# Attention followed by a two-layer MLP on one core: q and k turned by DMA for 33 pairs of heads, their loads moved from the SP queue to GpSimd's

## The chip, the cores and the metric

One core of one Trainium2 chip runs the whole program. The time is the device time of the program in microseconds (us). Three runs of the kernel before gave 479.93, 480.0 and 480.4 us, median 480.0 us. One more execution was profiled; all rows below come from it.

## The reference, cut to what matters

q, k and v are float32 of shape (8, 12, 448, 64): 8 batches, 12 heads, 448 positions, 64 columns.

```python
scores = (1/sqrt(64)) * q @ k^T
m = max(scores, -1);  e = exp(scores - m)
attn = e / (sum(e, -1) + exp(-m) + 1e-9)
x = (attn @ v), heads side by side      # (8*448, 768)
h = x @ w_in                            # (3584, 2048)
out = (h * tanh(softplus(h))) @ w_out   # (3584, 768), float32
```

## The kernel before, in words

**Pairs and units.** Work goes by pairs of heads: 48 pairs, 6 to a batch. Pairs 0 to 5 are a head part of their own (the loop `for p in range(HEAD)`, L618). From then on three pairs make a unit (`UNIT_PAIRS`, L16); the loop over units is L653, with u from 2 to 17. Unit u has the pairs p0 = 3u to 3u+2. Each unit has 12 steps (L664) and then 8 pieces of the first MLP matmul (the loop over f, L724).

**The life of a pair.** `load_pair` (L121) brings q, k and v of a pair from HBM, 224 KB each, as 112 partitions of 2 x 256 float32. `cast_pair` (L165) makes bfloat16 of q and k on GpSimd (L179, L180), `cast_v` (L185) of v (L188). `transpose_pair` (L190) turns q and k with eight TensorE instructions (L208, one block of 112 x 128 each) into PSUM. `evac_qk` (L221) takes them out: VectorE scales the two halves of q into `qd` (L254), ScalarE copies k into `kT` (L262). Then `scores` (L291): TensorE computes q k^T (L311), VectorE the negated maximum (L332), ScalarE the exponentials (`exps`, L345). `normalise` (L410) divides on VectorE, seven instructions a pair (L414), and turns the result `en` into `eT` with one DMA transpose on SP's queue (L422). `av_pair` (L445) multiplies by v on TensorE (L462) one unit later.

**MLP.** `mm1_mish` (L493) is the first layer with its activation, `mm2_part` (L523) the second, cut into chunks of two matmuls (L551) that fill the steps of the units from u = 4 on (`first_mm2`, L564). `store_rows` (L508) issues the output stores on SP's queue (L516).

**What sets the order.** The schedule is written out by hand: each engine executes its instructions in the order in which the program issues them, and so does each queue of DMAs. Within a unit:

- At the steps 0, 3 and 6 (`LOAD_AT`, L592) L689 to L694 load q and k of the pair four ahead (`LEAD` = 4, L591), load v of the next pair, cast q and k of the pair three ahead, and cast v of this pair. In the kernel before all these loads are on SP's queue, behind the DMA transposes and stores issued earlier.
- At the pieces f = 1, 3 and 5, L739 to L741 turn and evacuate q and k of the three pairs of the next unit. At f = 4, 6 and 7 the first three scores of the next unit are issued (L737, L742).
- At f = 0, 3 and 7, `normalise` divides the unit's three pairs and issues their three DMA transposes (L731, L744).
- `av_pair` of the last unit's three pairs goes with the last step of each pair (L305, L661).

**Weights.** `load_w` (L153) loads 20 pieces of w_in and w_out on GpSimd's queue, casting in the DMA. The last four pieces are issued in unit 4, after the steps 3, 5 and 7 (`W_AT`, L599). With `behind` it first makes GpSimd copy two elements (L157) that a pair's `eT` must hold, so that what follows waits for that DMA transpose.

**Times in the profile.** Unit 4 runs from about 97 to 123.51 us; unit 5 begins at 123.51, and each later unit 26.51 us after the last.

Of the kernel before, what the change touches and what calls it, by code (L numbers as in the profile page):

```python
# [10 lines left out]
BF16 = mybir.dt.bfloat16  # L11
# [4 lines left out]
UNIT_PAIRS = 3  # L16
# [3 lines left out]
def kernel(  # L20
# [9 lines left out]
    nc = tc.nc  # L30

    B, H, S, D = q.shape
# [3 lines left out]
    NT = 4  # L36
    SP_ = S // NT
    HP = H // 2
# [9 lines left out]
    N_PAIRS = B * HP  # L48
# [9 lines left out]
    PS = bass.MemoryType.PSUM  # L58
    singles = pool("singles", 1)
    ld_pool = pool("ld", 3)  # L60
    bf_pool = pool("bf", 4)
    qk_pool = pool("qk", 3)
    st_pool = pool("st", 5)
    hl_pool = pool("hl", 4)
    rb_pool = pool("rb", 2)
# [16 lines left out]
    w_in_sb = singles.tile([128, DM_T, d_ff], BF16)  # L82
    w_out_sb = singles.tile([128, FF_T, d_model], BF16)
    gT = singles.tile([128, FF_T, 2 * S], BF16)

    marks = singles.tile([1, 4, 16], BF16)
    N_EN = 5
# [30 lines left out]
    spread_copy = {}  # L118


    def load_pair(p, names="qkv"):  # L121
        if p >= N_PAIRS:
            return
        b, h0 = p // HP, (p % HP) * 2
        for nm in names:
            src = dict(q=q, k=k, v=v)[nm]
            t = ld_pool.tile([SP_, 2, NT * D], FP32, tag=f"{nm}_f", name=f"{nm}_f")
            nc.sync.dma_start(
                out=t, in_=src[b, h0 : h0 + 2].rearrange("h (p t) d -> p h (t d)", t=NT)
            )  # L130
            loaded.setdefault(p, {})[nm] = t
# [33 lines left out]
    def cast_pair(p, with_v=True):  # L165
        if p >= N_PAIRS:
            return
        q_f, k_f, v_f = (loaded[p].get(nm) for nm in "qkv")
        q_bf = bf_pool.tile([SP_, NT, 2, D], BF16, tag="q_bf", name="q_bf")
        k_bf = bf_pool.tile([SP_, NT, 2, D], BF16, tag="k_bf", name="k_bf")  # L170
        v_bf = bf_pool.tile([SP_, 2, NT * D], BF16, tag="v_bf", name="v_bf", bufs=12)
        by_t = "p h (t d) -> p t h d"
        q_t, k_t = (t.rearrange(by_t, t=NT) for t in (q_f, k_f))
        if p == 0:
            nc.vector.tensor_copy(out=k_bf, in_=k_t)
            for half in (slice(0, NT // 2), slice(NT // 2, NT)):
                nc.vector.tensor_copy(out=q_bf[:, half], in_=q_t[:, half])
        else:
            nc.gpsimd.tensor_copy(out=q_bf, in_=q_t)  # L179
            nc.gpsimd.tensor_copy(out=k_bf, in_=k_t)  # L180
        casted[p] = (q_bf, k_bf, v_bf)
        if with_v:
            cast_v(p)

    def cast_v(p):  # L185
        if p >= N_PAIRS:
            return
        nc.gpsimd.tensor_copy(out=casted[p][2], in_=loaded.pop(p)["v"])  # L188

    def transpose_pair(p, bank=None):  # L190
        if p >= N_PAIRS:
            return
        q_bf, k_bf, _ = casted[p]
        if bank is None:
            ps = mo_take()
            ps_k = mo_take() if p == 0 else ps
        else:
            ps, ps_k = sc_tiles[2 - bank][:, 0, :], sc_tiles[2 - bank][:, 1, :]
        by_s = [
            t[:, :].bitcast(BF16).rearrange("p (s n) -> p s n", s=2)[:, s, :]  # L200
            for s, t in enumerate((ps, ps_k))
        ]
        by_2 = sc_tiles[2][:, 0, :].bitcast(BF16)
        srcs = list(enumerate((q_bf, k_bf)))
        for s, src in reversed(srcs) if p == 0 else srcs:
            for t in range(NT):
                to = by_2 if p == 0 and s == 0 and t >= NT // 2 else by_s[s]
                nc.tensor.transpose(  # L208
                    to[:, t * SP_ : (t + 1) * SP_],
                    src[:, t].rearrange("p h d -> p (h d)"),  # L210
                    ident[:SP_, :SP_],
                )
        own = [] if bank is not None else [ps, ps_k] if p == 0 else [ps]
        qkT[p] = (by_s, own)
# [6 lines left out]
    def evac_qk(p, act=False):  # L221
        if p >= N_PAIRS:
            return
        (q_ps, k_ps), own = qkT[p]
        mo_free.extend(own)
        q_reads = []
        qd = q_diag[p % 3]
        kT = qk_pool.tile([128, S], BF16, tag="kT", name="kT")
        if p < DIAG_FROM:
            qT = qd.rearrange("d i h r -> d (i h r)")[:, 0:S]  # L230
            qkT[p] = (qT, kT)
            if p == 0:
                nc.scalar.copy(kT, k_ps[:, 0:S])
                by_2 = sc_tiles[2][:, 0, :].bitcast(BF16)
                for ps, half in (q_ps, slice(0, S // 2)), (by_2, slice(S // 2, S)):
                    nc.vector.tensor_scalar(
                        out=qT[:, half], in0=ps[:, half], scalar1=SCALE, scalar2=None,
                        op0=ALU.mult,
                    )
                return  # L240
            if act:
                nc.scalar.mul(qT, q_ps[:, 0:S], SCALE)
            else:
                q_reads.append(nc.vector.tensor_scalar(
                    out=qT, in0=q_ps[:, 0:S], scalar1=SCALE, scalar2=None, op0=ALU.mult
                ))
        else:
            qkT[p] = (qd, kT)
            if p < DIAG_FROM + 3:
                nc.vector.memset(qd[0:64, :, 1, :], 0.0)  # L250
                nc.vector.memset(qd[64:128, :, 0, :], 0.0)
            for h in range(2):
                rows = slice(64 * h, 64 * h + 64)
                q_reads.append(nc.vector.tensor_scalar(  # L254
                    out=qd[rows, :, h, :],
                    in0=q_ps[rows, 0:S].rearrange("d (i r) -> d i r", i=QB),
                    scalar1=SCALE, scalar2=None, op0=ALU.mult,
                ))
        if own and not act:
            nc.vector.tensor_copy(out=kT, in_=k_ps[:, 0:S])  # L260
        else:
            k_read = nc.scalar.copy(kT, k_ps[:, 0:S])  # L262
            if not own:
                apart(k_read, *q_reads)
# [326 lines left out]
    LEAD = UNIT_PAIRS + 1  # L591
    LOAD_AT = (0, 3, 6)  # L592
    HEAD = HP

    BY_PE = {HEAD - 1: 1, HEAD: -2, HEAD + 1: 2}
    AV_AT = {0: {1: 3, 5: 4, 8: 5}, 1: {1: 8, 4: 6, 8: 7}}
# [56 lines left out]
    for u in range(UNITS_PER_B, N_UNITS + 2 * UNITS_PER_B):  # L653
# [10 lines left out]
        for n in range(steps):  # L664
            pi, s = divmod(n, STEPS)
            p, idx = p0 + pi, p0 * STEPS + n
            late_tp = u == UNITS_PER_B and n == STEPS
            exps(idx)
            if u == UNITS_PER_B + 1 and n == 0:
                for j in range(2):  # L670
                    turn_on_pe(HEAD, j, busy_first=3)
            flush_late()
            if late_tp:
                transpose_pair(p0 + 2)
                evac_qk(p0 + 2)
            if held and n == 1:
                late.extend(held)
                held.clear()
                flush_late()
            late.extend(slow)  # L680
            slow.clear()
            acc += weight[n]
            want = int(total * acc / sum(weight) + 1e-6)
            while done < want:
                fn, w = filler.popleft()
                fn()
                done += w
            scores_ahead(end)
            if n in LOAD_AT:  # L689
                at = p0 + LOAD_AT.index(n)  # L690
                load_pair(at + LEAD, "qk")
                load_pair(at + 1, "v")
                cast_pair(at + LEAD - 1, with_v=False)
                cast_v(at)  # L694
            for pe, n0 in BY_PE.items():
                j = n - n0
                first = 2 if pe == HEAD else 0
                if pe // UNIT_PAIRS == u - 1 < first_mm2 - 1 and first <= j < NT:
                    turn_on_pe(pe, j, busy_first=1)
            spread = RDEN_AT.get(u - UNITS_PER_B, {})  # L700
            if n in spread:
                on_act = u < first_mm2
                spread_rden(
                    spread[n], copy=nc.scalar.copy if on_act else nc.vector.tensor_copy,
                    behind=slow if on_act else late,
                )
            early = AV_AT.get(u - UNITS_PER_B)
            if early is not None and n == 7:
                keep_busy(6, bank=mo_free[0])
            if early is not None:  # L710
                if n in early:
                    av_pair(early[n], half=p)
            elif s == (2 if pi else 0) and N_PAIRS <= p < N_PAIRS + UNIT_PAIRS:
                av_pair(p - UNIT_PAIRS)
            if u - UNITS_PER_B < len(W_AT):
                at = (u - UNITS_PER_B, n)
                load_w(W_AT[at[0]].get(n, 0), behind=W_BEHIND.get(at))
# [61 lines left out]
```

## Time and profile before

| | before |
|---|---|
| median of three runs | 480.0 us |
| the profiled execution, whole | 479.66 us |
| its span, first to last instruction | 477.9 us |
| TensorE busy | 458.8 us, 96% |
| VectorE busy | 358.7 us, 75% |
| ScalarE busy | 344.7 us, 72% |
| GpSimd busy | 103.8 us, 22% |
| mean granted TensorE clock | 0.996 |

The profiled execution lies 0.3 us below the median; 1.8 us of it lie outside the span. A row of the page's group part gives line, engine, operation, tiles, shapes and count, then busy time and mean duration, then the idle time of the engine just ahead and what ended it. PE is TensorE, DVE VectorE, ACT ScalarE, POOL GpSimd, SP SyncE. The DMA part counts packets: q1 is the queue of SP (hardware_dynamic), q0 that of GpSimd (software_dynamic).

### The profile page before, as it was taken

To read this page: it belongs to the slowest core of one execution; us is meant where nothing else is said; L and a number is where in the kernel's file an instruction comes from. 1 tells how busy PE (TensorE), PEld (TensorE's weight loads), DVE (VectorE), ACT (ScalarE), POOL (GpSimd) and SP (SyncE) were. 2 spreads that over 40 slices of the span, in tenths; PEclk is the share of its full clock that TensorE was granted. 3 is DMA by queue.
4 is the path that set the end of the run, shared out by engine and by line. 5 is a ranking of instruction groups with operands and counts; after the bars stand their busy time and mean duration, and the time that the engine had idled before them with its cause. 6 is when DMAs were issued, how large, how long until landed. Compare 5 with 4: busy or idle time off the path is not lost.

```text
span 477.9 us, 9363 instructions
## 1 busy us (share of the span) xinstructions
PE 458.8 (96%) x3291; PEld 257.8 (54%) x3291; DVE 358.7 (75%) x715; ACT 344.7 (72%) x907; POOL 103.8 (22%) x186
## 2 busy tenths in 40 slices
PE   6878999999999999999999999999999999999996
PEld 3344555555555565556555555555555555556563
DVE  5899849569898998889899979888898889421011
ACT  5998878788797868788787968687887978312300
POOL 3623536106031311304040312204040300000000
PEclk9999999999999999999999999999999999999999
DMA  8999999999999979898989999989989596961122
GB/s 215 227 224 213 234 222 183 185 212 233 195 301 207 261 149 214 211 198 227 192 229 171 267 156 260 198 192 231 190 220 198 173 181 156 156 142 34 34 63 71
DMA packets 204975, 91.09 MB, mean 191 GB/s; under 512 B 161792, under 2 KB 201472, under 8 KB 204928
## 3 DMA queue, kind: packets, MB, share of 16 engines
q1 hardware_dynamic: 197408, 84.18, 81.0%
q0 software_dynamic: 7488, 6.29, 8.8%
q8 instruction: 26, 0.43, 0.4%
q14 instruction: 21, 0.17, 0.1%
q10 hardware_dynamic: 32, 0.02, 0.0%
HBM read 45.61 MB, written 11.01 MB: 118 GB/s over the span
## 4 chain that ended last, share of the span: by engine, by line
PE 69%; DVE 8%; ACT 6%; issue 1%; DVEq 0%
PE mo L498 24%; PE mo L551 24%; PE sc L311 7%; ACT en L345 6%; PE sc L462 6%; DVE negm L332 5%; PE sc L498 3%; PE sc L208 3%; DVE en L414 1%; DVE xT L475 1%; PE mo L462 1%; DVE o_sb L534 1%; PE mo L272 0%; DVE eT L437 0%; ACT L345 0%
## 5 line engine op out<-in xcount | busy, mean ns | idle before, releaser
L345 ACT ACTIVATE en<-sc,negm 128x448 bf16<-128x448 f32 x336 | 208.7, 640 | 22.5 <-DVE negm L332 20.7
L332 DVE TENSOR_REDUCE negm<-sc 128x2 f32<-128x896 f32 x192 | 182.6, 970 | 39.6 <-PE sc L311 29.3
L551 PE MATMUL mo<-w_out_sb,gT 128*128 128x384 bf16 (+1 forms) x1024 | 166.8, 307 | 0.4 <-DVE rb L402 0.4
L498 PE MATMUL mo<-xT,w_in_sb 128*128 128x448 bf16 x672 | 141.9, 353 | 0.3 <-DVE xT L475 0.3
L551 PEld LDWEIGHTS <-gT 128*128 128x128 bf16 x1024 | 96.3, 98 | 56.0 <-issue 1.9
L504 ACT ACTIVATE gT<-mo 128x448 bf16<-128x448 f32 x112 | 59.3, 543 | 78.9 <-PE mo L498 78.6
L498 PEld LDWEIGHTS <-w_in_sb 128*128 128x128 bf16 x768 | 72.7, 98 | 63.4 <-issue 3.2
L179 POOL CAST q_bf<-q_f 112x512 bf16<-112x512 f32 x47 | 29.9, 635 | 222.1 <-DMA q_f<-in_q_dram 196.1
L414 DVE TENSOR_SCALAR en<-en,rden 128x448 bf16<-128x448 bf16 x252 | 74.2, 367 | 0.8
L311 PE MATMUL sc<-kT,qd 128*128 128x448 bf16 x252 | 71.6, 354 | 0.1
L345 ACT ACTIVATION_READ_ACCUMULATOR en<-sc,negm 128x1 f32 x336 | 71.0, 211 | 0.0
L534 DVE COPY o_sb<-mo 128x384 f32<-128x384 f32 (+1 forms) x64 | 31.8, 497 | 48.3 <-PE mo L551 48.1
L462 PE MATMUL sc<-eT,v_bf 112*64 112x448 bf16 x336 | 39.8, 357 | 1.4 <-ACT en L345 0.9
L311 PEld LDWEIGHTS <-qd 128*128 128x128 bf16 x252 | 24.4, 97 | 29.0 <-issue 12.9
L188 POOL CAST v_bf<-v_f 112x512 bf16<-112x512 f32 x48 | 29.9, 624 | 31.5 <-DMA v_f<-in_v_dram 31.4
L254 DVE TENSOR_SCALAR qd<-sc 64x448 bf16<-64x448 bf16 x72 | 27.7, 385 | 6.2 <-PE sc L208 5.4
L462 PEld LDWEIGHTS <-v_bf 112*64 112x64 bf16 x384 | 20.0, 109 | 20.0 <-issue 11.6
L180 POOL CAST k_bf<-k_f 112x512 bf16<-112x512 f32 x47 | 29.2, 622 | 6.1 <-DMA k_f<-in_k_dram 3.5
L262 ACT COPY kT<-sc 128x448 bf16<-128x448 bf16 x39 | 20.8, 534 | 0.6 <-PE sc L208 0.6
L498 PE MATMUL sc<-xT,w_in_sb 128*128 128x448 bf16 x96 | 20.8, 353 | 0.0
L475 DVE CAST xT<-sc 128x448 bf16<-128x448 f32 x33 | 20.3, 614 | 0.0
L208 PEld LDWEIGHTS <-q_bf 112*128 112x128 bf16 x192 | 13.7, 99 | 10.0 <-POOL q_bf L179 2.0
(61 smaller groups left out, 278.9 us busy)
## 6 DMA issues: line engine op xcount, KB each, us to landing
k_f<-in_k_dram SPq DMA_DIRECT2D x48, 224.0 KB, 5.2
q_f<-in_q_dram SPq DMA_DIRECT2D x48, 224.0 KB, 5.2
v_f<-in_v_dram SPq DMA_DIRECT2D x48, 224.0 KB, 5.5
w_in_sb<-in_moe_w_in_dram POOLq DMA_DIRECT2D x12, 256.0 KB, 8.7
w_out_sb<-in_moe_w_out_dram POOLq DMA_DIRECT2D x8, 384.0 KB, 10.1
out_dram<-o_sb SPq DMA_DIRECT2D x7, 336.0 KB, 3.7
out_dram<-o_sb SPq DMA_DIRECT2D x8, 288.0 KB, 4.8
out_dram<-o_sb SPq DMA_DIRECT2D x8, 240.0 KB, 3.4
```

The source lines that it names most:

```text
L179: nc.gpsimd.tensor_copy(out=q_bf, in_=q_t)
L180: nc.gpsimd.tensor_copy(out=k_bf, in_=k_t)
L188: nc.gpsimd.tensor_copy(out=casted[p][2], in_=loaded.pop(p)["v"])
L311: nc.tensor.matmul(sc[:, bk, 0:S], lhsT=qT[:, i].rearrange("d h r -> d (h r)"), rhs=kT, start=True, stop=True,)
L332: half_max[p] = nc.vector.tensor_reduce(out=negm, in_=sc[:, 0 : len(cols), 0:S], axis=AX.X, op=ALU.max, negate=True)
L345: e = nc.scalar.activation(out=st["en"][:, :, c, 0:SP_], in_=sc[:, bk, 0:S].rearrange("q (j c) -> q j c", j=NT), func=AF.Exp, bias=st["neg ...
L414: nc.vector.tensor_scalar(out=en[:, :, i, 0:SP_], in0=en[:, :, i, 0:SP_], scalar1=st["rden"][:, i : i + 1], scalar2=None, op0=ALU.mult,)
L462: mm = nc.tensor.matmul(av[h * 64 : (h + 1) * 64, 0:S], lhsT=v_bf[:, h, j * D : (j + 1) * D], rhs=e_h, start=(j == 0), stop=(j == NT - 1),)
L498: nc.tensor.matmul(h_ps[:, 0:S], lhsT=w_in_sb[:, dm, ff * 128 : (ff + 1) * 128], rhs=xT[b][:, dm, :], start=(dm == 0), stop=(dm == DM_T - 1),)
L504: nc.scalar.activation(out=gT[:, ff, b % 2 * S : b % 2 * S + S], in_=h_ps[:, 0:S], func=AF.Mish)
L534: nc.vector.tensor_copy(out=o_sb[:, cols.start : cols.start + n_dve], in_=st["o"][:, 0:n_dve])
L551: nc.tensor.matmul(st["o"][:, 0:n_cols], lhsT=gT[:, ff, i * 128 : (i + 1) * 128], rhs=w_out_sb[:, ff, cols], start=(ff == 0), stop=(ff == ...
```

## The change

From pair 15 on (`QK_BY_DMA_FROM`) q and k are no longer turned on TensorE. Their bfloat16 copies go to two fixed tiles for three pairs, `q_cast` and `k_cast`, and at step 6 of each unit two DMA transposes on SP's queue, one for k and one for q, turn the three pairs of the next unit into `kT_all` (room for two units) and `qT_all` (one unit). `evac_qk` then scales q from `qT_all` in SBUF, and k is not copied at all.

From unit 4 on the loads of q and k are issued from GpSimd's queue, and v is neither loaded as float32 nor cast by an instruction: one DMA from GpSimd's queue loads and casts it. At the start of unit 4, GpSimd first waits for `eT` of pair 10. The buffers of `v_bf` go from 12 to 8.

```diff
-    bf_pool = pool("bf", 4)
-    qk_pool = pool("qk", 3)
+    bf_pool = pool("bf", 3)
...
+    q_cast, k_cast = (
+        singles.tile([SP_, UNIT_PAIRS, NT, 2, D], BF16, tag=f"{nm}_cast", name=f"{nm}_cast")
+        for nm in "qk"
+    )
+    kT_all = singles.tile([128, 2 * UNIT_PAIRS, S], BF16)
+    qT_all = singles.tile([128, UNIT_PAIRS, S], BF16)
...
-    def load_pair(p, names="qkv"):
+    def load_pair(p, names="qkv", queue=None):
...
-            nc.sync.dma_start(
+            (queue or nc.sync).dma_start(
...
-        nc.gpsimd.tensor_copy(out=casted[p][2], in_=loaded.pop(p)["v"])
+        v_bf = bf_pool.tile([SP_, 2, NT * D], BF16, tag="v_bf", name="v_bf", bufs=8)
+        if "v" in loaded[p]:
+            nc.gpsimd.tensor_copy(out=v_bf, in_=loaded.pop(p)["v"])
+        else:
+            b, h0 = p // HP, (p % HP) * 2
+            nc.gpsimd.dma_start(
+                out=v_bf, in_=v[b, h0 : h0 + 2].rearrange("h (p t) d -> p h (t d)", t=NT)
+            )
+        casted[p][2] = v_bf
+
+    def turn_qk_by_dma(p):
+        if not QK_BY_DMA_FROM <= p < N_PAIRS:
+            return
+        at = p % (2 * UNIT_PAIRS)
+        for to, src in (kT_all[:, at : at + UNIT_PAIRS], k_cast), (qT_all, q_cast):
+            nc.sync.dma_start_transpose(
+                out=to.rearrange("d g (t p) -> d (g t) p", t=NT),
+                in_=src.rearrange("p g t h d -> p (g t h d)"),
+            )
...
     def transpose_pair(p, bank=None):
-        if p >= N_PAIRS:
+        if p >= N_PAIRS or p >= QK_BY_DMA_FROM:
             return
...
+        by_dma = p >= QK_BY_DMA_FROM
+        kT = kT_all[:, p % (2 * UNIT_PAIRS)]
+        (q_ps, k_ps), own = ((qT_all[:, p % UNIT_PAIRS], kT), []) if by_dma else qkT[p]
...
+        if by_dma:
+            return
...
+    QK_BY_DMA_FROM = 2 * HP + UNIT_PAIRS
...
                 at = p0 + LOAD_AT.index(n)
-                load_pair(at + LEAD, "qk")
-                load_pair(at + 1, "v")
+                by_pool = u >= first_mm2
+                if u == first_mm2 and n == 0:
+                    load_w(0, behind=p0 - 2)
+                load_pair(at + LEAD, "qk", queue=nc.gpsimd if by_pool else None)
+                if not by_pool:
+                    load_pair(at + 1, "v")
                 cast_pair(at + LEAD - 1, with_v=False)
+                if n == LOAD_AT[-1]:
+                    turn_qk_by_dma(p0 + UNIT_PAIRS)
                 cast_v(at)
```

More of the change, by code (lines that the diff above doesn't have):

```diff
@@ L167, in cast_pair @@
             return
[L168 to L171, printed above, removed]
+        q_f, k_f = (loaded[p][nm] for nm in "qk")
+        q_bf, k_bf = q_cast[:, p % UNIT_PAIRS], k_cast[:, p % UNIT_PAIRS]
         by_t = "p h (t d) -> p t h d"
@@ L180, in cast_pair @@
             nc.gpsimd.tensor_copy(out=k_bf, in_=k_t)
-        casted[p] = (q_bf, k_bf, v_bf)
+        casted[p] = [q_bf, k_bf, None]
         if with_v:
@@ L223, in evac_qk @@
             return
-        (q_ps, k_ps), own = qkT[p]
+        by_dma = p >= QK_BY_DMA_FROM
+        kT = kT_all[:, p % (2 * UNIT_PAIRS)]
+        (q_ps, k_ps), own = ((qT_all[:, p % UNIT_PAIRS], kT), []) if by_dma else qkT[p]
         mo_free.extend(own)
@@ L227, in evac_qk @@
         qd = q_diag[p % 3]
-        kT = qk_pool.tile([128, S], BF16, tag="kT", name="kT")
         if p < DIAG_FROM:
```

## Prediction

> **What bounds the kernel now.** I read the shares first, then the chain that ended last, then one stage after the other, and last the queues.
>
> ```profile
> PE 458.8 (96%) x3291; PEld 257.8 (54%) x3291; DVE 358.7 (75%) x715; ACT 344.7 (72%) x907; POOL 103.8 (22%) x186
> ...
> PE 69%; DVE 8%; ACT 6%; issue 1%; DVEq 0%
> ```
>
> TensorE is busy for 96% of the span and holds 69% of the chain. In the units the share is higher still. The table by stage gives for unit 9:
>
> ```profile
> 229.55:256.06 26.51, 26.51 (x183) 14.84 (x181) 23.74 (x48) 21.59 (x57) 5.44 (x9) 1.00 0.91 206
> ```
>
> TensorE is busy for all 26.51 us at the full clock, VectorE for 23.74, ScalarE for 21.59, GpSimd for 5.44. So from unit 5 on a TensorE instruction less is time less, as long as nothing that TensorE waits for comes later. The timeline of TensorE shows what the change takes out:
>
> ```profile
> 249.43 0.36 PE L208 MATMUL sc<-ident,q_bf 112*128 112x112 bf16 x4
> 249.63 0.36 PE L208 MATMUL sc<-ident,k_bf 112*128 112x112 bf16 x4
> 249.82 1.30 PE L498 MATMUL mo<-xT,w_in_sb 128*128 128x448 bf16 x6
> 250.96 0.54 PE L311 MATMUL sc<-kT,qd 128*128 128x448 bf16 x2
> ```
>
> The eight instructions of a pair hold TensorE from 249.43 to 249.82, 0.39 us (the row of 213 ns each counts overlapping ends). Next, what shares the DMA engines. From 84 to 93 us a DMA transpose ran while weights came over GpSimd's queue; the DMA view of that stretch says:
>
> ```profile
> q0 software_dynamic: 1713, 1.28, 90.5%
> q1 hardware_dynamic: 1713, 0.44, 36.4%
> ```
>
> Both queues moved exactly 1713 packets in 9 us: one against one, 190 a microsecond each. Alone, the transpose moves 2538 in the 3 us from 252 to 255, 846 a microsecond, and 1130 where a backlog had formed (2267 from 63 to 65). So beside a GpSimd load a transpose falls to less than a quarter. In the kernel before this is rare: q, k and v stand on SP's own queue, where nothing runs against the transposes from about 122 us on.
>
> **What goes.** TensorE: 33 pairs (15 to 47) x 0.395 us = **-13.0 us**, all on the path in units 4 to 14. The order of the two programs shows 264 matmuls fewer, 33 x 8, so that part is certain. ScalarE loses 33 copies of k (534 ns each, 17.6 us), off the path: it idles 4.9 us per unit. VectorE scales q from SBUF instead of PSUM; the nearest row for SBUF is L414 with a pitch of 0.245 us against 0.39 for L254. That is 66 x 0.14 = 9 us of VectorE, hidden by TensorE. GpSimd loses 36 casts of v (624 ns), off the path by themselves. SP loses its loads, so its transposes no longer hold loads back.
>
> **What comes: the DMA transposes of q and k.** No row shows 12 blocks of 112 x 128. An `eT` of 28 blocks takes SP 4.25 us and lands 6.1 us after its start when alone. By blocks, a new one takes 1.8 us and lands after 3.6. If the time does not depend on the number of blocks, it takes 4.0 us (the shortest one of 21 blocks, 4.02). I take 1.8, since the 28 blocks flow at an even 217 GB/s. Two in a row, after the last store ahead of them on SP's queue (7 to 12 us into the unit by VectorE's copies L534), land 14 to 19 us into it; `evac_qk` needs them at about 18 to 20. That just fits, with nothing beside it.
>
> **Unit 4, where it does not fit.** GpSimd waits for pair 10's `eT`, issued at 91.99 and landed at 101.2. Then it has, ahead of the last cast of pair 17: four loads of q and k behind it (0.75 us each by L162's rows of 742 to 762 ns), one cast of v, six casts (0.62), one DMA for v, two weight pieces, two more loads: about 11 us, so SP can issue the new transposes at 112.6. On GpSimd's queue there then stand half of two weight pieces (450 packets), a pair of loads (448), and behind them v (224), two weight pieces (1024) and the next pair of loads (448): some 2,600 packets. The two transposes have 2 x 12 x 112 = 2,688. One against one at 190 a microsecond that is 14 us: q lands near 127. VectorE waits for it, and TensorE wants the first scores of unit 5 at 118.40 - 0.8 = 117.6. The stall is 1.5 us if nothing shared the engines, 11 us by this count. I take **+9 us**, once.
>
> **Units 5 to 13: two new waits.** GpSimd may overwrite `q_cast` only when the transpose of the unit before has landed. So its whole section starts at about 14 to 19 us into a unit, just when VectorE divides and `eT` is transposed.
>
> (a) `eT` of the first pair starts at 250.20 and lands at 256.42; its matmul L462 comes at 259.3 (232.75 + 26.51), 2.9 us later, and 1.7 once the unit is 1.2 shorter. Nine loads of 224 packets now run on GpSimd's queue in some 12 us. Five of them meet this transpose and take 0.8 us each (224 KB at 275 GB/s, the rate of SP's loads from 66 to 68); the slack between 846 and 1130 packets per microsecond gives back 1. It lands 3 us late: a stall of 1.3 us. Bounds: 0, and 4 if all nine meet it.
>
> (b) VectorE and GpSimd hold each other up. Alone the seven divisions take 1.81 us (251.69 to 253.50); with casts beside them 2.2 to 3.2. Beside weight loads, GpSimd's timeline has
>
> ```profile
> 113.23 1.49 POOL L162 DMA_DIRECT2D w_out_sb<-in_moe_w_out_dram  x2
> 114.70 0.64 POOL L179 CAST q_bf<-q_f 112x512 bf16<-112x512 f32 x1
> ```
>
> and on VectorE's timeline
>
> ```profile
> 113.91 3.73 DVE L414 TENSOR_SCALAR en<-en,rden 128x448 bf16<-128x448 bf16 x7
> ```
>
> The first of these seven took 1.56 us, until both DMA issues and the cast were over. After the change GpSimd has 6 casts and 9 issues per unit, 10.4 us instead of 5.4, in this very place. Nine VectorE instructions lie between the sum's reciprocal and the first scores; alternating with GpSimd's they take 9 x 0.65 = 5.9 us where 3.3 are free: a stall of up to 2.6, or none where GpSimd's section begins later. I take 0.6.
>
> The Trainium skill ("SBUF — State Buffer", "Who interferes with whom") says that VectorE in a two-port mode and GpSimd lock each other out of a shared port for a whole instruction, and that whoever is first wins. The row above agrees on the lock, with VectorE as the loser. The page also names the other loser, descriptor writing starved by VectorE; that is a rival below. On the queues the same skill ("DMA: Bandwidth & Descriptors", "Queues, rings and completion order") says that each DMA engine takes turns between queues by packets; the 1713 against 1713 above is what it looks like here.
>
> Nine units x (1.3 + 0.6) = **+17.1 us**. The sum: 479.7 - 13.0 + 9 + 17.1 = 492.8, and with the 0.3 us up to the median **493 us**.
>
> **The rivals.**
>
> - *Late transposes as above* (chance 0.45): 485 to 503.
> - *VectorE starved* (0.18): it gets one instruction in per GpSimd instruction through the whole section. The second pair's division then ends 8 us later; its `eT` starts 30 us after the unit's start instead of 24, lands at 37 and is needed at 33.4. A stall of 3.5 to 4 us per unit, with about 1 of (b): 479.7 - 13 + 9 + 9 x 4.5 = 516. For it: the 1.56 us. Against it: the mean of L414 is 0.367 us against 0.33 alone, although casts meet it today, and GpSimd's waits for its own loads leave gaps.
> - *Faster, TensorE stays the bound* (0.24): the new transposes of unit 4 get through early and the loads are over before `eT` starts. The place is the queue of unit 4 and the first `eT` of each unit; it decides at whether q lands before about 118 us and each first `eT` within 28.5 us of the unit's start. Then 479.7 - 13.0 + 1.5 to 5 = 468 to 472, 467 with no stall at all. For it: loads come a unit ahead of need, and SP is free of them.
> - *GpSimd is the loser* (0.10): its issues wait for VectorE, at most 1.8 us behind seven divisions, and the loads have a unit in hand. (b) is nothing: 493 - 5.4 = 487.6.
> - *The terms cancel* (0.03): 479 to 481.
>
> That the transposes stay on TensorE is excluded by the count above.
>
> **The numbers.** The range runs from 467 (no stall anywhere) to 514; what is left out is the worst of the starved case and, below, next to nothing. The likeliest case alone spans 485 to 503. A measurement of this kernel can tell 0.2% from no change: faster 0.24, same 0.03, slower 0.73.
>
> **What would show it.** L208 down from 384 matmuls to 120, and the gap of 0.39 us between L498 groups gone. In unit 4, an idle of TensorE before L311 of 5 us or more, ended by VectorE's `qd`, which itself waited for the DMA into `qT_all`. From unit 5 on, idle time of TensorE before L462 that ends with a DMA into `eT`, and DMA transposes whose time on SP grows from 4.25 to 5 us and more. For (b), a mean of L414 above 0.37 us. It would be wrong if unit 4 shows no such idle, or if the units take 25.3 us; and too low if L414 goes to 0.6.

## The result, and the profile after

The changed kernel takes 524.3 us (median of six executions, 523.7 to 534.6) against 480.0: a ratio of **1.093**, 95% interval 1.090 to 1.095. Forecast were 493 us and a range of 467 to 514. Medians below are over all executions and ratios leave disturbed ones out, so that the two need not match. The rows of "after" are those of one more execution of 521.0 us, span 519.2 (e0 below).

First the shares and the chain that ended last, as they were read before:

```profile
PE 457.1 (88%) x3027; PEld 247.2 (48%) x3027; DVE 370.7 (71%) x715; ACT 331.9 (64%) x874; POOL 146.3 (28%) x251
...
PE 41%; DMA 29%; DVE 8%; ACT 4%; issue 1%; POOL 1%; SPq 1%; DVEq 0%; POOLq 0%
```

The 264 matmuls are gone (3291 to 3027), yet TensorE is busy for 88% instead of 96%, and DMA, which had no share worth a line, holds 29% of the chain. Where TensorE stands idle is told by the group part (busy, mean | idle just before, and what ended it):

```profile
L336 PE MATMUL sc<-kT_all,qd 128*128 128x448 bf16 x252 | 74.1, 365 | 16.5 <-DVE qd L277 16.5
L439 DVE TENSOR_SCALAR en<-en,rden 128x448 bf16<-128x448 bf16 x252 | 87.6, 418 | 0.9
...
L487 PE MATMUL sc<-eT,v_bf 112*64 112x448 bf16 x336 | 42.8, 377 | 27.4 <-DMA eT<-en 26.0
```

The same rows of the kernel before:

```profile
L414 DVE TENSOR_SCALAR en<-en,rden 128x448 bf16<-128x448 bf16 x252 | 74.2, 367 | 0.8
L311 PE MATMUL sc<-kT,qd 128*128 128x448 bf16 x252 | 71.6, 354 | 0.1
...
L462 PE MATMUL sc<-eT,v_bf 112*64 112x448 bf16 x336 | 39.8, 357 | 1.4 <-ACT en L345 0.9
```

L336 are the scores (L311 before), L487 the attention matmul (L462 before), L439 the divisions (L414 before). So 16.5 us are lost ahead of the scores and 27.4 ahead of the attention matmul. Nearly all of the first lot is one stall in unit 4. TensorE's timeline (start, length, engine, line, operation, tiles, count, idle before and what ended it):

```profile
115.68 2.43 PE L523 MATMUL mo<-xT,w_in_sb 128*128 128x448 bf16 x12
133.07 0.93 PE L336 MATMUL sc<-kT_all,qd 128*128 128x448 bf16 x2 [14.96 <-DVE qd L277]
133.79 3.62 PE L523 MATMUL mo<-xT,w_in_sb 128*128 128x448 bf16 x12
```
SP's queue at the same time:
```profile
112.56 3.68 SPq L207 DMA_TRANSPOSE kT_all<-k_cast  x1
116.28 6.62 SPq L207 DMA_TRANSPOSE qT_all<-q_cast  x1
123.08 19.40 SPq L447 DMA_TRANSPOSE eT<-en  x2
```
And VectorE:
```profile
132.23 1.58 DVE L277 TENSOR_SCALAR qd<-qT_all 64x448 bf16<-64x448 bf16 x4 [15.63 <-DMA qT_all<-q_cast]
```

SP issues the new transposes at 112.56 and 116.28; q lands at 132.2, 15.9 us after its start; VectorE scales it, and TensorE goes on at 133.07 after 14.96 us. Twelve L523 matmuls then take 3.62 us where twelve took 2.43 before the stall: the granted clock is at 0.50 from 122.5 to 136.2 us.

Most of the second lot comes in pieces of 1.3 to 5.4 us, nearly one a unit. The table by stage gives unit 6 and unit 8 (busy time of PE, PEld, DVE, ACT, POOL, then clock, DMA, GB/s):

```profile
168.00:196.30 28.30, 25.52 (x167) 14.41 (x166) 25.33 (x48) 20.39 (x54) 12.32 (x20) 1.00 1.05 210
...
223.10:254.70 31.60, 27.43 (x167) 14.91 (x165) 24.64 (x49) 20.58 (x53) 12.17 (x20) 0.89 1.05 204
```

TensorE's own work is 25.5 us, 1.0 less than before; but unit 6 lasts 28.3 and unit 8 lasts 31.6, where the clock is lowered as well (0.89 on the mean, and 27.43 us for the same work). What TensorE's timeline has in unit 8:

```profile
228.86 0.81 PE L576 MATMUL mo<-w_out_sb,gT 128*128 128x384 bf16 x4
233.84 1.70 PE L487 MATMUL sc<-eT,v_bf 112*64 112x448 bf16 x8 [4.17 <-DMA eT<-en]
```

The `eT` it waits for was issued at 220.26 and landed 13.4 us later; before the change an `eT` landed after 6.1 to 8.4. Meanwhile GpSimd's queue held loads issued from 216.63 to 225.47.

All kernels below are read in the same way. Unit 4 and units 5 to 14 are measured from the first exponentials of a unit to those of the next; the idle columns are those of the rows of the scores and of the attention matmul, over the whole run, in us. All columns but the median are of one profiled execution.

| kernel | median | unit 4 | units 5-14 | idle, scores | idle, attention |
|---|---|---|---|---|---|
| before | 480.0 | 27.1 | 265.1 | 0.1 | 1.4 |
| after | 524.3 | 42.4 | 290.4 | 16.5 | 27.4 |
| e1 turning alone | 498.5 | 40.6 | 270.8 | 28.7 | 1.5 |
| e2 loads alone | 522.5 | 26.8 | 309.4 | 0.0 | 37.4 |
| e3 after, from pair 18 | 521.8 | 26.8 | 314.2 | 1.3 | 44.6 |
| f1 turning alone, from 18 | 489.1 | 26.8 | 277.6 | 18.3 | 1.5 |
| f2 = f1, loads ahead on SP | 483.8 | 26.8 | 262.3 | 0.0 | 9.8 |
| f3 = f2, loads on GpSimd's queue | 553.1 | 26.8 | 316.9 | 2.4 | 50.7 |
| f4 = f3, GpSimd waits for `eT` | 539.9 | 26.8 | 325.4 | 48.8 | 7.0 |

(The profiled executions took 499.7 us for e1, 527.9 for e2, 532.4 for e3, 494.5 for f1, 478.5 for f2, 530.6 for f3 and 540.9 for f4. The other three of f3 took 553 to 554.)

### The profile page after: what moved, and what is told of

It reads as the page before. It is cut to its first block, busy times and chain, and to the rows that moved or that the text cites. A ratio compares the mean times of both kernels' runs of the same rounds, so it can differ in the third digit from the quotient of the medians.

```text
span 532.8 us, 8727 instructions
## 1 busy us (share of the span) xinstructions
PE 463.2 (87%) x3027; PEld 249.5 (47%) x3027; DVE 370.7 (70%) x715; ACT 332.3 (62%) x874; POOL 145.8 (27%) x251
## 3 DMA queue, kind: packets, MB, share of 16 engines
q0 software_dynamic: 21008, 24.99, 25.4%
## 4 chain that ended last, share of the span: by engine, by line
PE 37%; DMA 28%; DVE 10%; ACT 4%; POOL 2%; SPq 2%; issue 2%; DVEq 0%; POOLq 0%
DMA eT<-en 20%; PE mo L576 13%; PE mo L523 12%; PE sc L487 4%; DVE negm L357 4%; PE sc L336 4%; DMA qT_all<-q_cast 4%; ACT en L370 4%; DVE en L439 3%; DMA q_f<-in_q_dram 3%; PE sc L523 2%; DMA out_dram<-o_sb 2%; SPq L207 1%; DVE o_sb L559 1%; SPq L447 1%
## 5 line engine op out<-in xcount | busy, mean ns | idle before, releaser
L576 PE MATMUL mo<-w_out_sb,gT 128*128 128x384 bf16 (+1 forms) x1024 | 170.7, 311 | 0.4 <-DVE rb L427 0.4
L523 PE MATMUL mo<-xT,w_in_sb 128*128 128x448 bf16 x672 | 140.8, 356 | 3.1 <-DMA w_in_sb<-in_moe_w_in_dram 2.8
L523 PEld LDWEIGHTS <-w_in_sb 128*128 128x128 bf16 x768 | 74.8, 99 | 74.7 <-issue 6.6
L336 PE MATMUL sc<-kT_all,qd 128*128 128x448 bf16 x252 | 74.9, 368 | 19.2 <-DVE qd L277 19.2
L183 POOL CAST q_cast<-q_f 112x512 bf16<-112x512 f32 x47 | 29.3, 624 | 214.7 <-DMA qT_all<-q_cast 194.0
L439 DVE TENSOR_SCALAR en<-en,rden 128x448 bf16<-128x448 bf16 x252 | 87.0, 416 | 0.9
L487 PE MATMUL sc<-eT,v_bf 112*64 112x448 bf16 x336 | 42.8, 377 | 31.9 <-DMA eT<-en 24.2
L336 PEld LDWEIGHTS <-qd 128*128 128x128 bf16 x252 | 24.7, 100 | 52.1 <-DVE qd L277 22.0
L487 PEld LDWEIGHTS <-v_bf 112*64 112x64 bf16 x384 | 21.1, 112 | 51.5 <-issue 37.2
L277 DVE TENSOR_SCALAR qd<-qT_all 64x448 bf16<-64x448 bf16 x66 | 24.9, 377 | 18.8 <-DMA qT_all<-q_cast 18.0
L184 POOL CAST k_cast<-k_f 112x512 bf16<-112x512 f32 x47 | 29.9, 637 | 2.0 <-DMA k_f<-in_k_dram 1.6
L197 POOL DMA_DIRECT2D v_bf<-in_v_dram x35 | 23.2, 662 | 9.1 <-PE sc L336 8.5
L134 POOL DMA_DIRECT2D q_f<-in_q_dram x32 | 21.4, 669 | 0.1
L134 POOL DMA_DIRECT2D k_f<-in_k_dram x32 | 21.4, 669 | 0.0
L523 PE MATMUL sc<-xT,w_in_sb 128*128 128x448 bf16 x96 | 20.8, 352 | 0.0
```

The costliest lines, as they stand in the source:

```text
L134: (queue or nc.sync).dma_start(out=t, in_=src[b, h0 : h0 + 2].rearrange("h (p t) d -> p h (t d)", t=NT))
L336: nc.tensor.matmul(sc[:, bk, 0:S], lhsT=qT[:, i].rearrange("d h r -> d (h r)"), rhs=kT, start=True, stop=True,)
L439: nc.vector.tensor_scalar(out=en[:, :, i, 0:SP_], in0=en[:, :, i, 0:SP_], scalar1=st["rden"][:, i : i + 1], scalar2=None, op0=ALU.mult,)
L487: mm = nc.tensor.matmul(av[h * 64 : (h + 1) * 64, 0:S], lhsT=v_bf[:, h, j * D : (j + 1) * D], rhs=e_h, start=(j == 0), stop=(j == NT - 1),)
L523: nc.tensor.matmul(h_ps[:, 0:S], lhsT=w_in_sb[:, dm, ff * 128 : (ff + 1) * 128], rhs=xT[b][:, dm, :], start=(dm == 0), stop=(dm == DM_T - 1),)
L576: nc.tensor.matmul(st["o"][:, 0:n_cols], lhsT=gT[:, ff, i * 128 : (i + 1) * 128], rhs=w_out_sb[:, ff, cols], start=(ff == 0), stop=(ff == ...
```

## The experiments

Two theories at first. **A:** loads on GpSimd's queue and DMA transposes on SP's hold each other up in the DMA engines. **B:** it is the two added transposes per unit on SP's own queue.

**e0, the changed kernel again.** 

> The changed kernel once more, unchanged. Every theory expects 523 to 525 us. If its profile shows the stalls of the first one in the same places (TensorE idle some 17 us ahead of the first scores of unit 5, 1 to 5 us ahead of the first attention matmul of most later units, with the granted clock at 0.5 behind the long ones), these belong to the kernel and not to one execution.


521.0 us, 2 us under what was expected, with the stalls in the same places: the rows above.

**e1, the turning alone.**
```diff
-                by_pool = u >= first_mm2
+                by_pool = False
```


> q and k are turned by DMA from pair 15 on, but their loads stay on SP's queue and v is loaded and cast as before. Theory A (what is late is late because loads on GpSimd's queue take turns with the DMA transposes on the DMA engines): from unit 5 on eT lands within 7 us of its start again and the idle ahead of the attention matmul goes; in unit 4 the four weight pieces still run beside the new transposes, a stall of 2 to 10 us: 467 + 2 to 10 and as much again for the clock, 469 to 480 us. Theory B (the two more DMA transposes per unit are what delays eT, on SP's own queue): the idle ahead of the attention matmul stays, 2 to 3 us a unit and as much again for the clock, 495 to 520 us.


498.5 us, ratio 1.037 (1.030 to 1.044): above what A expected, at the lower end of B's. The idle ahead of the attention matmul is gone (1.5 us), as A had it and against B. But 13.0 us stand ahead of the first scores of unit 5, with no load of q, k or v on GpSimd's queue: only the last four pieces of w_out. And 0.9 to 2.4 us stand ahead of the scores in every later unit, which neither had: SP reaches the turning only behind three `eT` and nine loads (in unit 5 the loads run from 144.0, the turning starts at 153.0, its last block lands at 158.8).

**e2, the loads alone.**
```diff
-    QK_BY_DMA_FROM = 2 * HP + UNIT_PAIRS
+    QK_BY_DMA_FROM = N_PAIRS
```


> q and k of all pairs are turned on TensorE as before; the loads of q and k from unit 4 on are on GpSimd's queue and v is cast in its DMA there. Theory A: eT lands 8 to 14 us after its start as in the changed kernel; TensorE has 13 us more to do in units 4 to 14, which is slack for eT (1.2 us a unit), so of the 2.7 us idle a unit 1.5 stay, with the clock 480 + 9 x 1.5 to 3, 490 to 507 us, and no stall ahead of the first scores of unit 5. Theory B: eT is in time, and the time is that of the kernel before, 478 to 483 us.


522.5 us, ratio 1.084 (1.077 to 1.092): nearly the whole loss without one DMA transpose added. B is out as the main cause. A's count was too small, too: 37.4 us idle, 12.5 of them in unit 5, ahead of the attention matmul:

```profile
142.92 1.70 PE L487 MATMUL sc<-eT,v_bf 112*64 112x448 bf16 x8 [12.48 <-DMA eT<-en]
```

So the jam of unit 4 (the last weight pieces and the loads of q, k and v) hits whichever transpose is next: that of q in the changed kernel, the first `eT` here (issued at 120.4, landed at 142.9).

**e3, the changed kernel from pair 18 on** (`QK_BY_DMA_FROM = 2 * HP + 2 * UNIT_PAIRS`).


> The changed kernel, but q and k are turned by DMA from pair 18 on, so the first such transposes come in unit 5, when all weights are in. Theory A, in the form that the four weight pieces of unit 4 make its stall: the stall of 17.6 us ahead of the first scores of unit 5 goes and does not come back a unit later (1 to 3 us at most); with 1.2 us more for TensorE and the clock no longer halved there (about 10 us), 495 to 503 us. Rival (the stall is that of the first such transposes wherever they come, by the loads of q, k and v alone): it stands ahead of the first scores of unit 6 and the time stays at 520 to 526 us. Theory of the clock: the granted clock keeps at 1.0 up to the first idle of over 3 us.


521.8 us, ratio 1.084 (1.078 to 1.090). A missed: the stall leaves the scores, and 13.1 us of it come back ahead of the attention matmul of unit 5, as in e2. It was neither the first turning as such, as the rival had it, nor gone.

**f1, e1 from pair 18 on** (both edits above).


> As the run with the turning alone (loads on SP's queue, v cast by instruction), but turned by DMA from pair 18 on. Theory A (the stall of 13 us ahead of the first scores of unit 5 is that of two DMA transposes beside the last four weight pieces, and of nothing else): 498.5 - 13 - 1.7 for the halved clock behind it + 1.2 for three pairs turned on TensorE again = 485, from 482 to 489 us; the idles of 1 to 2.3 us ahead of the scores of the later units stay, as SP still issues the transposes of q and k behind three eT and nine loads. Rival (the first DMA turning stalls wherever it comes): 496 to 501 us.


489.1 us, ratio 1.016 (1.011 to 1.021), the upper edge of what was expected. Unit 4 falls from 40.6 to 26.8 us; 3.7 us stand ahead of the scores in the unit after. With no load on GpSimd's queue the weight pieces meet no turning and the jam is gone. The 1 to 3 us a unit ahead of the scores stay.

**f2, f1 with nine loads ahead, on SP's queue.** From unit 5 on:
```diff
-                load_pair(at + LEAD, "qk", ...)
-                    load_pair(at + 1, "v")
                 cast_pair(at + LEAD - 1, with_v=False)
                 if n == LOAD_AT[-1]:
                     turn_qk_by_dma(p0 + UNIT_PAIRS)
                 cast_v(at)
+                if n == LOAD_AT[-1] and u >= first_mm2:
+                    queue = None
+                    for j in range(0 if ahead else 1, UNIT_PAIRS):
+                        load_pair(p0 + 2 * UNIT_PAIRS + j, "qk", queue)
+                        load_pair(p0 + UNIT_PAIRS + j, "v", queue)
```


> As the last one, but from unit 5 on the nine loads of a unit stand on SP's queue behind the transposes of q and k, and one unit further ahead (q and k of the pairs 6 to 8 after the unit's first, v of the pairs 3 to 5 after it). Theory A (what is late in the steady units is the order on SP's queue): no idle over 0.5 us ahead of the scores or the attention matmul, 480 - 30 pairs x 0.395 = 468, from 466 to 473 us, faster than the kernel before. Rival (SP's queue has too much to issue: three eT at 4.2 us, two turns at 1.5, nine loads and eight stores at 0.45 are 23.3 of 25.3 us): eT comes late, 475 to 490 us.


483.8 us (477.0 to 488.6), ratio 0.998 (0.995 to 1.001). The wait ahead of the scores is gone (0.0 us), so the order on SP's queue had made it. But 9.8 us ahead of the attention matmul stay, and units 5 to 14 take 262.3 us where 253.2 would be due (265.1 - 11.9): no measurable gain over the kernel before. That is within what the rival expected.

**f3, f2 with the same loads on GpSimd's queue.** One line:
```diff
-                    queue = None
+                    queue = nc.gpsimd if ahead else None
```


> The last kernel with one thing different: from unit 5 on the nine loads, at the same place of the program and as far ahead, go through GpSimd's queue. Theory A (loads on a second queue beside DMA transposes cost more than their own bytes, whatever their order): eT lands 8 to 13 us after its start, idles of 1 to 5 us ahead of the attention matmul, 488 to 512 us. Rival (not the queue but the order was at fault, the loads held until q and k are turned): 466 to 474 us as on SP's queue.


553.1 us (530.6 to 554.0): 69 us above f2 by the medians, and its fastest execution is 42 above f2's slowest. The order in the program is the same, and one queue differs. The moment differs with it. In units 5 to 13 SP issues f2's loads 12 to 20 us into a unit. GpSimd issues f3's as soon as a turning has landed and nine casts are done (186 us of its idle time end with that landing), from 23 us into a unit to 3 us into the next, which is when the `eT` run. So in units 5 to 14 a load is in flight beside 22 of 30 `eT`, against 9 of 31 in f2. Where one is, an `eT` lands after 11.7 us on the mean (8.3 in f2), and while both are in flight the DMA engines move 214 GB/s (287 in f2). Where none is, it lands after 5.8 us (6.1 in f2).

Single stretches of 8 us differ widely. The DMA view of f2 from 226 to 234 us, whose loads and transposes stand on one queue (q1):

```profile
DMA packets 5089, 2.31 MB, mean 288 GB/s; under 512 B 4090, under 2 KB 4960, under 8 KB 5088
```
Of f3 from 156 to 164 us, with the slowest of all `eT` under way (21.9 us):

```profile
DMA packets 2845, 1.04 MB, mean 130 GB/s; under 512 B 2753, under 2 KB 2753, under 8 KB 2844
...
q1 hardware_dynamic: 2727, 0.70, 95.2%
q0 software_dynamic: 117, 0.32, 34.7%
```
And of f3 from 325.5 to 333.5 us, with an `eT` under way that lands after 14.5 us:

```profile
DMA packets 3635, 2.70 MB, mean 337 GB/s; under 512 B 3094, under 2 KB 3094, under 8 KB 3635
...
q0 software_dynamic: 669, 1.94, 70.3%
q1 hardware_dynamic: 2966, 0.75, 44.4%
```

In both stretches of f3 the transposes' queue moves 341 and 371 packets per us, where it moved 846 alone. In the first, the loads hardly move either; in the second, they move most of the bytes. So an `eT` beside these loads is late in both cases, but the two queues don't always move less together. Theory A's size was still too small (488 to 512 expected), and since the loads also came at another moment, f2 and f3 don't tell the queue from the moment.

**f4, f3 with GpSimd waiting for the third `eT` of the unit before.**
```diff
+                    if ahead and u < N_UNITS - 1:
+                        load_w(0, behind=p0 - 1)
```


> The last kernel, but GpSimd copies two elements of the eT of the third pair of the unit before ahead of the nine loads, so that they start when this DMA transpose has landed and run in the 8 to 10 us before the next one. Theory A: the loads no longer meet an eT for most of their time; idles fall to under 1 us, 467 to 478 us. Rival (GpSimd's nine DMA issues cost VectorE its divisions, wherever they are): the division's mean stays at 0.40 us or above and the time stays within 5 us of the last kernel's.


539.9 us (528.4 to 541.5), and by the fastest executions (528.4 against f3's 530.6) no gain. A missed by 60 us, for a reason that helps it: when that `eT` lands, SP starts the two turnings, and now these meet the nine loads. Their mean landing goes from 4.3 to 9.9 us, the idle ahead of the attention matmul from 50.7 to 7.0, that ahead of the scores from 2.4 to 48.8:

```profile
L336 PE MATMUL sc<-kT_all,qd 128*128 128x448 bf16 x252 | 75.3, 371 | 48.8 <-DVE qd L277 48.1
L439 DVE TENSOR_SCALAR en<-en,rden 128x448 bf16<-128x448 bf16 x252 | 86.9, 416 | 1.0
...
L487 PE MATMUL sc<-eT,v_bf 112*64 112x448 bf16 x336 | 40.6, 362 | 7.0 <-DMA eT<-en 4.2
```

The rival expected a time within 5 us of f3's: the medians are 13 apart, the fastest executions 2. The division's mean stays at 0.42 us, as it had it, but these rows show no idle of TensorE that ends with a division: divisions slowed beside GpSimd are there and cost little.

**g1, f2 with the loads on ScalarE's queue** (`queue = nc.scalar if ahead else None`).


> As the kernel with the nine loads of a unit ahead on SP's queue (483.8 us), but these loads are issued from ScalarE's queue, at the same place of the program. Theory A1 (any second queue whose packets stand beside a DMA transpose does it): eT lands 10 to 20 us after its start as with GpSimd's queue, 510 to 555 us. Theory A2 (it is GpSimd's queue, with its packets of 4096 bytes): eT lands within 9 us, 478 to 495 us, including up to 6 us a unit of issuing on ScalarE, which idles about 7 us a unit.


565.0 us, ratio 1.171 (1.165 to 1.177), and it doesn't tell A1 from A2. `eT` lands in 5.5 us on the mean, for the loads run earlier, and 27 of 31 `eT` have none in flight beside them; the turnings, which they meet, land in 8.4. Most of the loss is another wait: of 71.3 us idle ahead of the scores 70.8 end with the exponentials. The loads stand in ScalarE's own order, and where one waits for its buffer the exponentials wait, too.

```profile
147.63 0.32 ACTq L134 DMA_DIRECT2D v_f<-in_v_dram  x1
148.00 0.64 ACT L370 ACTIVATE en<-sc,negm 128x448 bf16<-128x448 f32 x1 [7.34 <-DMA k_f<-in_k_dram]
```

**g2, f2 with only the three loads of v on GpSimd's queue.**


> The kernel with nine loads a unit on GpSimd's queue (553 us) against the one with all on SP's queue (484 us): here only the three loads of v go through GpSimd's queue, q and k stay on SP's. Theory A with a price per load: a third of 69 us, 484 + 23 = 507, from 497 to 517 us, and eT that meets a load lands 3 us later per load met. Rival (a few loads fit beside a transpose, the price comes only with a backlog): 478 to 492 us.


488.7 us, ratio 1.016 (1.013 to 1.020): against f2, three loads cost 5 us by the medians and 9 by the ratios; nine cost 69, or 47 in f3's fastest execution. That is less than a third of either, so not a price per load; the time is in the rival's range. With three, `eT` lands after 7.8 us on the mean (6.6 in f2, 9.6 in f3, where single ones took 21.9).

**g3, f3 with each load split into even and odd partitions.**


> The kernel with nine loads a unit on GpSimd's queue, each load split in two (even and odd partitions), so that its packets are 1024 bytes and not 4096; 18 issues a unit. Theory A2 (long packets hold each DMA engine's transposing packets up): the packets take some 60 to 100 ns instead of 234, eT lands 3 us or more sooner than in that kernel, 495 to 525 us. Theory A1 (every turn counts, whatever its size): four times as many turns, 540 to 580 us.


526.5 us, ratio 1.093 (1.088 to 1.099). The packets in the record are still of 4096 bytes (4704 of them), so the edit didn't do what it was for; and f3's own executions differ by nearly as much. Nothing follows on the size of packets.

**g4, f2 with four dummy matmuls instead of two in the head.**


> The kernel with nine loads ahead on SP's queue, with four instead of two dummy matmuls behind each of the first three steps of the six head pairs. Its profile had lost 6.25 us of TensorE work in the head to a halved clock, the kernel before 1.55. If the dummies keep the clock up, the time falls to 470 to 476 us and the runs agree within 1%; if the halved clock comes from something else, 477 to 489 us as without them.


482.1 us, ratio 1.004 (1.001 to 1.006). The clock stays at 1.00 through the head, as meant, and the time does not fall: the halved clock in the head was not what kept f2 from its 468.

**h1, f2 with k alone turned by DMA,** q on TensorE; **h2, f2 with the loads of v behind the unit's first `eT`; h3, the new buffers alone** (`QK_BY_DMA_FROM = N_PAIRS`, `by_pool = False`, no wait for pair 10's `eT`).


> The kernel with nine loads ahead on SP's queue, but only k is turned by DMA; q is turned on TensorE as before. If the DMA engines had become the bound (24 of 25.3 us a unit), 1.5 us a unit is given back and TensorE has 0.6 us a unit more: no stalls, 480 - 30 x 0.2 = 474, from 472 to 478 us. If they had not, it is slower than that kernel by what TensorE does more, or as scattered as it is: 480 to 490 us.

> The kernel with nine loads ahead on SP's queue, but the three loads of v are issued behind the first eT of the unit and not ahead of it. If only the order on SP's ring delays the first eT (its issue takes 5 to 6.6 us there, 3.5 alone), it is issued in under 5 us, the idles of 1 to 2 us ahead of the attention matmul go, and the time falls by 4 to 8 us, to 474 to 480. If the DMA engines are full, the second and third eT are late instead: 481 to 490 us.

> The changed kernel with its new buffers (fixed tiles of three pairs for the casts of q and k, six slots for kT, eight buffers for v) and nothing else of the change: q and k turned on TensorE, all loads on SP's queue, v cast by an instruction. If the buffers are neutral: 478.5 to 481 us, runs within 0.3%. If the head loses more to the halved clock because of them: 482 to 486 us, scattered by 1%.


h1: 483.1 us, ratio 1.004 (1.001 to 1.007). The idle in units 5 to 14 halves (8.8 to 4.2 us), as with DMA engines relieved, but TensorE has 7 us more to do, and unit 4 of the profiled execution a stall of 2 us: no gain, the number was missed. h2: 485.1 us, ratio 1.007 (1.004 to 1.011): loading v later gives nothing, so it isn't the order alone. h3: 480.3 us, ratio 1.000 (0.998 to 1.002): the buffers are neutral, though this execution, too, lost 4.8 us of TensorE work to a halved clock in the head, 1.6 before.

What f2 then lacks is told by the table by stage, for one of its units without a stall:

```profile
258.10:283.60 25.50, 25.40 (x167) 14.44 (x166) 24.18 (x50) 20.24 (x54) 5.55 (x9) 1.00 1.12 241
```

In this unit TensorE is the bound again, at 25.5 us, and 241 GB/s have to be moved at a DMA share of 1.12; in the kernel before it was 206 at 0.91, in 26.51 us. The units of f2 take 25.4 to 27.6 us. That the DMA engines are nearly the bound there, so that a small delay is not made up, is argued from this and fits h1 and h2. No run shows it by itself, and single stretches of 8 us move more: 304 GB/s in f2 (325.5 to 333.5 us), 337 in f3.

## Why the prediction was wrong

By stage, the profiled executions differ by 41.3 us in their spans: 0.4 up to unit 4, 15.3 in unit 4, 25.3 in units 5 to 14. By what TensorE did, with the forecast beside it (us; work is busy time at the full clock, and lost work is busy time by one minus the granted clock):

| term | forecast | measured |
|---|---|---|
| TensorE's work | -13.0 | -12.1 |
| the stall ahead of the first scores of unit 5 | +9 | +15.0 |
| (a), ahead of the attention matmul of a unit's first pair | +11.7 | +12.1 |
| the same ahead of its second pair | nothing | +14.0 |
| (b), ahead of the other scores | +5.4 | +1.5 |
| work lost to the lowered clock behind the idles | nothing | +10.3 |
| together, with 0.5 of rest | +13.1 | +41.3 |

So of the 28 us that were missed, 24 are two terms that the prediction put at nothing, and 6 are the size of unit 4; the other differences nearly cancel.

- **TensorE, -13.0: right.** The matmuls went down by 264. The work fell by 12.1 us, from 26.5 to some 25.4 a unit.
- **VectorE, 9 us less for scaling q: not there.** L277 takes 377 ns where L254 took 385. It was off the path.
- **The DMA transposes of q and k, 1.8 and 3.6 us: right.** From unit 5 on they take SP 1.4 to 2.6 us and land after 4.1 on the mean.
- **Unit 4, +9: the mechanism right, the size too small.** SP issued at 112.56, forecast 112.6; the scores waited for `qd`, and that for the DMA into `qT_all`, as said. But q landed at 132.2, not 127: 14.96 us idle and 1.6 of lowered clock. The rule of one packet against one at 190 per us was the fault. From 118 to 126 us the view of the DMA has

```profile
DMA packets 1901, 0.89 MB, mean 112 GB/s; under 512 B 1221, under 2 KB 1874, under 8 KB 1901
...
q0 software_dynamic: 701, 0.59, 85.7%
q1 hardware_dynamic: 1200, 0.30, 63.3%
```

  150 packets per us for the transposes and 88 for the loads, 112 GB/s in all. The 190 came from one stretch of the kernel before (191 GB/s in all). There a packet of the loads took 76 ns and one of the transposes 31, by the shares of its rows; here they take 156 and 68. Why is open. In e1, with some 2,000 packets (four pieces of 512) on GpSimd's queue, the same count gives 11 us for the two transposes (2,000 at 190, the other 700 at 1130); from 112.1 to 130.2 they took 18. The stretch from 118 to 124 us of e1:

```profile
DMA packets 1090, 0.45 MB, mean 75 GB/s; under 512 B 753, under 2 KB 1090, under 8 KB 1090
```

- **(a), 1.3 us a unit: right for the transpose that it priced; the step that failed is that it priced only the first `eT` of a unit.** In units 5 to 13 the first `eT` lands after 10.0 us on the mean against 6.6 before: 3.4 us late, where 3 were forecast. Packets of GpSimd's queue fill the 16 engines for 4.6 us of that time, where five loads at 0.8 us are 4. The idle is 12.1 us against 11.7; so close a hit is luck in part, for the first profiled execution (534.6 us) has 17.9. But the loads met the second `eT` as well. It lands after 10.6 us against 6.5, and TensorE idles 14.0 us ahead of its matmul (12.6 in the execution of 534.6 us), for which the sum has no term (the rival of the starved VectorE had a late second pair, by another cause). The third lands after 7.0 us, as before. The 4.17 us shown above are such a wait for a second `eT`. The DMA view of its time, 220.3 to 233.7 us:

```profile
DMA packets 6494, 3.06 MB, mean 228 GB/s; under 512 B 5438, under 2 KB 6110, under 8 KB 6494
...
q1 hardware_dynamic: 5294, 1.34, 68.2%
q0 software_dynamic: 1200, 1.72, 55.1%
```

  The loads moved 1.72 MB, as much as 7.5 loads of 224 KB, and filled the engines for 7.4 us (55.1% of 13.4); the `eT` landed 7.3 us later than the 6.1 of one alone. So a load cost about its own time here, as the prediction had it. What it had wrong is how many transposes the loads meet.
- **The clock: a term that was missing.** Every idle of more than 3.5 us in units 5 to 14, in the rows of after, is followed by 3.4 to 6.9 us at a granted clock of 0.50 (behind 4.17 us idle at 229.7, from 231.7 to 238.6); those of 1.3 to 2.0 are not. It cost 8.7 us there and 1.6 in unit 4. The Trainium skill ("TensorE: Matmul & The Clock Gate", "HAM oscillation") says that idles over some 3.4 us throttle the clock again; the rows of after agree. Other traces differ: single idles of 2.0 us did it in e2 and h1, and one of 3.72 us in e2 did not.
- **(b), 0.6 us a unit: not there.** The divisions are slower beside GpSimd (L439 at 418 ns; 334 in e1, whose loads are on SP), but only 16.5 - 14.96 = 1.5 us of idle ahead of the scores are left for it in the whole run. VectorE starved was wrong for the same reason: L439 did not go to 0.6. GpSimd was not the loser either: its issues of loads took 0.67 us on the mean.
- **The rival "faster"** fell at its own two points: q landed at 132, after 118, and the first `eT` were late.

All that the prediction named as its signs came: the idle ahead of the scores in unit 4, ended by `qd`; the idle ahead of the attention matmul, ended by `eT`; transposes that take SP up to 10 us; divisions above 0.37 us. The mechanism was right. The sum left out the second `eT` and the clock, and made the stall of unit 4 too small.

That the loads' move to GpSimd's queue makes `eT` late is shown by e1 and e2. The Trainium skill ("DMA: Bandwidth & Descriptors", "Rules for kernel authors") says, in a row on transposes that spoil each other's data, that a transpose next to ordinary DMAs needs nothing; it says nothing of time there. In time it is not free here: 11.7 us against 5.8 for an `eT` of f3. Why both queues together move so little in some stretches (75 GB/s in e1, 112 in the changed kernel, 130 in f3) and 228 to 337 in others stays open. The records do not tell on which DMA engine a packet ran; that a transpose moves in step on all of them, so that a foreign packet on one holds up the others, would fit the slow stretches, but it is only argued, and the fast ones speak against it as a rule. Also open: why f3 takes 530 in one execution and 553 in three. Not tried: the whole change with the last weight pieces loaded before unit 4, and loads on GpSimd's queue at the moment at which SP issues them in f2.

## What to carry to other kernels

Before traffic is moved to a second queue, list every transfer that it will meet in a unit, not only the first one on the path, and price each: here the second `eT` cost as much as the first. Ask when the new queue will issue, too: GpSimd's loads stood behind its casts and came just when the `eT` ran. Loads on the same queue as the transposes, behind them and far enough ahead of their use, kept the time of the kernel before (f2), but did not beat it. And price an idle of several microseconds on TensorE with the lowered clock behind it: here a quarter of the loss.

## What the runs showed of the hardware that was not expected

- An `eT` on SP's queue landed after 11.7 us on the mean where loads on GpSimd's queue were in flight (f3), after 8.3 where loads on SP's own queue were (f2), and after 5.8 to 6.1 where none was. While both were in flight, 214 GB/s were moved on two queues and 287 on one; stretches of 8 us of f3 reach from 130 to 337.
- Loads of 224 KB on GpSimd's queue go mostly as packets of 4096 bytes, on SP's as packets of 1024; splitting them by partitions did not change that.
- A halved clock in the head (1.6 to 6.3 us of work lost, from one execution to the next) need not show in the time: h3's profiled execution lost 4.8 us of work there against 1.6 before, and reached unit 4 only 0.5 us later.
- f2 scatters more than the kernel before: from 477.0 to 488.6 us in ten executions, against 478.7 to 482.3 in 21. That this is so because its time hangs on the DMA engines and not on TensorE is argued.
